# Shorter decay scans, 112-row loads, and eight small steps moved from VectorE to ScalarE and TensorE in a three-layer kernel

## The chip, the cores and the metric

The kernel runs on one core of a Trainium2 chip. Its time is the device time of one execution in microseconds; a run gives several, and the median is quoted. One execution was also recorded by the hardware profiler. The engines are TensorE (PE in the rows; PEld is its weight loading), VectorE (DVE), ScalarE (ACT), GpSimd (POOL) and SyncE (SP); each works through its own queue in order and waits for others by semaphores. SyncE and GpSimd issue the transfers here.

## The reference

```
for t in range(S):                     # layer 1: B=4, H=8, S=768, D=48
    state = alpha[t] * state + outer(k[t], v[t])
    y[t]  = q[t] @ state
x     = y, heads side by side          # [4, 768, 384]
theta = x @ w_theta                    # layer 2
u     = x + w_tok_r @ (x * cos(theta)) + w_tok_i @ (x * sin(theta))
x     = u + relu(u @ w_ch)
h     = relu(x @ w_in)                 # layer 3: 1024 columns
g, v  = h[:, :512], h[:, 512:]
v_s   = w_spatial @ normalise(v) + b_spatial
out   = (g * v_s) @ w_out
```

## The kernel before

The sequence is cut into units of 128 positions, six for each of four batches, so 24 units; a unit holds two chunks of 64 positions, and four pairs of heads lie side by side in the partitions (2 x 48 of 112 rows). For each unit, layer 1 is done in chunk form. `load_al` and `load_qk` bring the decays and q, k; `load_v` brings v. `att_scan` (L357 to L361) makes running products of the decays with two scans, one backwards into `rt` and one forwards in place, each over the 8 x 67 = 536 columns of a line in which a fixed column separates the groups; a reciprocal between them sets the forward scan's starting values. `att_qk` multiplies q and k by these products. TensorE then makes the products inside a chunk (`att_a`, tiles `psa`), which VectorE masks into `ax` and `am` (`att_mask`); `ax` is moved to the other half of the partitions by two transfers into `ay`. `att_k` and `att_kt` turn k, `att_u` makes each chunk's addition to the state, `att_y` the output. The state goes through VectorE chunk by chunk: `att_s` (L434) scales it by the chunk's decay (`ss` <- `tmp`), `att_t` (L447) adds the new part (`tmp` <- `psu`, `ss`). From unit 6 on `att_y` of a unit and `att_u` of the next are one joined TensorE step (`psuy`).

Layer 2 follows unit by unit. `tr_p` turns the output, `th_p` makes theta in turns (`th`, a PSUM tile). `th_k` (L541, ScalarE) adds a magic number that rounds to whole turns (`kk`), `th_r` (L551, VectorE) takes them off (`r`), and `th_a` and `th_s` (ScalarE) make the absolute value, sine and cosine (`z`). `z_m` multiplies them by x; for unit 0 it writes `zs` itself (L572), and that unit's accumulation uses unsplit f32 operands (`wf`). `tokmix` (L610) adds a unit's part to the five accumulators `acc0` to `acc4` of its batch; `acc1` is shared by two pieces and is set to zero first (`acc_zero`, L619). When a batch is complete, `ch_p` and its neighbours do the channel product. Layer 3 comes after unit 23.

Large operands are split into a high and a low part in a 32-bit matmul format. The weights come as 64-bit numbers in pieces (`raw`, two buffers, issued by GpSimd at first), and each piece passes ScalarE (`top`, writes `zeros`), VectorE (`join`, writes `wf`, L248), ScalarE (`high`, L259) and VectorE (`low`, L267). A new piece is loaded when a `raw` buffer has been joined.

All steps of all three layers stand in one hand-set sequence: `ORDER` is a table of step numbers, and each engine's queue is that sequence cut down to its own steps. The code also holds switches that were empty before: `THP` is a set of units for which `th_n`, `th_m` and the negated identity replace `th_r`.

## Time and profile before

| | us |
|---|---|
| median of 3 runs | 585.23 |
| lowest, highest | 584.65, 585.68 |
| profiled execution, its own time | 585.29 |
| its span in the trace | 583.5 |
| TensorE busy | 561.5 (96%) |
| VectorE busy | 440.3 (75%) |
| ScalarE busy | 252.5 (43%) |

The time of an execution is a little longer than the span of its instructions. Busy time of an engine is the time in which at least one of its instructions is recorded as running; matmuls are pipelined, so their records overlap and a busy TensorE may still be waiting a little inside. A share over the whole span mixes the three layers, so the stretches matter more than the total. The granted TensorE clock was 1.00, 2.4 GHz, in the whole span.

### The profile page before, as it was taken

The page shows a single profiled execution, that of the slowest core. Times are in us where ns is not written, and L with a number is a line of the kernel's source. Part 1 is how long each engine was busy: PE and PEld are TensorE (multiplying, and loading weights), DVE is VectorE, ACT ScalarE, POOL GpSimd, SP SyncE. Part 2 cuts the span into 40 slices and gives each one's busy share as a digit, 9 for nine tenths or more (in the row PEclk, how much of TensorE's full clock was granted, in tenths as well). Part 3 has the DMA queues.
Part 4 walks back from the last instruction along what each step waited for, and adds up shares of the span by engine and source line. Part 5 has one row for each costly group of instructions (what it writes and reads, how often), then busy time and mean ns, then how long its engine had stood idle before and what let it go on. Part 6 is the DMA issues. An engine that isn't in the chain of part 4 may idle for free.

```text
span 583.5 us, 13445 instructions
## 1 busy us (share of the span) xinstructions
PE 561.5 (96%) x5737; PEld 510.4 (87%) x5737; DVE 440.3 (75%) x769; ACT 252.5 (43%) x474; POOL 25.1 (4%) x45
## 2 busy tenths in 40 slices
PE   1799999999999999999999999999999999999997
PEld 1666878888988889988989899999999899989997
DVE  6999999988788876878756887776665775767470
ACT  2476755435335433334554443534323441343232
POOL 1101100000000000000000100000000100011000
PEclk9999999999999999999999999999999999999999
DMA  8878756363253324333344525001002010211002
GB/s 287 295 240 278 245 184 215 112 198 126 86 169 110 104 88 128 122 104 97 95 139 168 180 89 183 1 0 62 20 2 95 29 41 0 82 42 40 1 1 81
DMA packets 28220, 66.23 MB, mean 114 GB/s; under 512 B 3073, under 2 KB 14337, under 8 KB 27905
## 3 DMA queue, kind: packets, MB, share of 16 engines
q1 hardware_dynamic: 25984, 53.51, 27.7%
q0 software_dynamic: 2176, 11.86, 5.9%
q8 instruction: 45, 0.74, 0.5%
q14 instruction: 15, 0.11, 0.1%
HBM read 52.78 MB, written 9.44 MB: 107 GB/s over the span
## 4 chain that ended last, share of the span: by engine, by line
PE 79%; DVE 10%; DMA 4%; ACT 2%; issue 2%; POOL 1%; DVEq 0%; SPq 0%; POOLq 0%; ACTq 0%
PE acc L610 22%; PE acc L929 11%; PE pu L861 8%; PE psc L652 7%; PE po L987 7%; PE psv L788 6%; PE sp L900 4%; PE th L534 3%; PE psuy L466 3%; DMA raw<-in_w 3%; PE th L537 2%; PE psa L383 2%; PE psuy L424 2%; PE psk L407 1%; DVE wf L248 1%
## 5 line engine op out<-in xcount | busy, mean ns | idle before, releaser
L610 PE MATMUL acc<-w,zs 128*128 128x256 f32 (+1 forms) x828 | 165.2, 344 | 0.0
L610 PEld LDWEIGHTS acc<-w,zs 128*128 128x128 f32 x828 | 128.0, 188 | 15.4
L788 PE MATMUL psv<-w,xs 128*128 128x512 f32 x216 | 53.7, 395 | 0.0
L987 PE MATMUL po<-w,gs 128*128 128x384 f32 x288 | 52.8, 338 | 0.3 <-ACT v L799 0.3
L861 PE MATMUL pu<-xs,w 128*128 128x384 f32 x288 | 53.0, 336 | 0.0
L987 PEld LDWEIGHTS po<-w,gs 128*128 128x128 f32 x288 | 50.7, 188 | 1.6 <-ACT v L799 0.7
L861 PEld LDWEIGHTS pu<-xs,w 128*128 128x128 f32 x288 | 50.3, 188 | 0.7 <-ACT o L997 0.2
L788 PEld LDWEIGHTS psv<-w,xs 128*128 128x128 f32 x216 | 40.0, 187 | 8.2 <-ACT v L799 0.2
L652 PE MATMUL psc<-us,wch 128*128 128x384 f32 (+1 forms) x243 | 41.2, 320 | 0.0
L652 PEld LDWEIGHTS psc<-us,wch 128*128 128x128 f32 x243 | 37.8, 189 | 0.8
L541 ACT ACTIVATE kk<-th,magic 128x384 f32<-128x384 f32 x24 | 13.9, 578 | 53.3 <-PE th L537 53.3
L973 ACT CAST gs<-t 128x384 fp32r<-128x384 f32 x32 | 15.8, 513 | 48.3 <-DVE t L966 48.3
L811 POOL TENSOR_TENSOR rs<-rs,mhalf 128x1 f32<-128x1 f32 x24 | 15.6, 652 | 441.7 <-DVE rs L808 441.7
L357 DVE TENSOR_TENSOR_SCAN al<-al,heads 112x536 f32<-112x536 f32 x24 | 30.5, 1270 | 3.3 <-DMA al<-in_al 3.3
L534 PE MATMUL th<-wth,xh 128*128 128x384 f32 x144 | 31.1, 352 | 0.9 <-ACT xh L501 0.5
L361 DVE TENSOR_TENSOR_SCAN al<-al,heads 112x536 f32<-112x536 f32 x24 | 30.6, 1275 | 0.8
L369 DVE TENSOR_TENSOR qk<-qk,al 112x1024 f32<-112x1024 f32 x24 | 29.3, 1220 | 2.1 <-DMA qk<-in_qk 2.1
L929 PE MATMUL acc<-w,mx 128*128 128x384 f32 x162 | 30.7, 338 | 0.0
L929 PE MATMUL acc<-wt,vns 128*128 128x384 f32 x162 | 30.7, 338 | 0.0
L929 PEld LDWEIGHTS acc<-wt,vns 128*128 128x128 f32 x162 | 28.6, 188 | 0.1
L929 PEld LDWEIGHTS acc<-w,mx 128*128 128x128 f32 x162 | 28.6, 188 | 0.0
L534 PEld LDWEIGHTS th<-wth,xh 128*128 128x128 f32 x144 | 25.4, 194 | 2.6 <-ACT xh L501 2.0
(122 smaller groups left out, 977.5 us busy)
## 6 DMA issues: line engine op xcount, KB each, us to landing
qk<-in_qk SPq DMA_DIRECT2D x24, 512.0 KB, 4.7
raw<-in_w POOLq DMA_DIRECT2D x14, 772.0 KB, 6.4
...
raw<-in_w SPq DMA_DIRECT2D x6, 772.0 KB, 5.5
...
```

The source lines that it names most:

```text
L357: nc.vector.tensor_tensor_scan(out=back[:, ::-1], data0=line[:, ::-1], data1=one[:, ::-1], initial=1.0, op0=ALU.mult, op1=ALU.add)
L361: nc.vector.tensor_tensor_scan(out=line, data0=line, data1=one, initial=0.0, op0=ALU.mult, op1=ALU.add)
L369: nc.vector.tensor_tensor(out=x, in0=x, in1=st[u]["ar"], op=ALU.mult)
L466: nc.tensor.matmul(psy[par][64 * c:64 * c + 64, a, :], w, v, start=part == 0 or first, stop=part == 1,)
L534: nc.tensor.matmul(th, xh[:, 0, k], wth[:, pr, k], start=(k == 0 and pr == 0), stop=False)
L610: nc.tensor.matmul(acc[b, n][:, c0:c1], zs[:, pl, ri, m * 128:(m + 1) * 128], w[:, pr, t0:t1], start=first and n != 1, stop=last, skip_gro ...
L652: nc.tensor.matmul(ps, wch[:, pl, k, m * 128:(m + 1) * 128], us[:, pr, k], start=(n == 0), stop=(n == 3 * KD - 1),)
L788: nc.tensor.matmul(ps, xs2[:, pl, k, o:o + 128], win[pr, "v"][:, k], start=(n == 0), stop=(n == 3 * KD - 1),)
L861: nc.tensor.matmul(pu, win[f // 2][:, pl, k * 256 + f % 2 * 128:k * 256 + f % 2 * 128 + 128], xq[b, h][:, pr, k], start=(n == 0), stop=(n ...
L900: nc.tensor.matmul(sp[:, :TH], vns[b, s][:, pl, f * 128:(f + 1) * 128], wsp[s][:, pr, t], start=(n == 0), stop=(n == 3 * NS - 1),)
L929: nc.tensor.matmul(g, left(b, n, j, pl, c), right(n, j, pr), start=(n in (1, 5, 6) and i == 0), stop=(i == 3 * NJ - 1), skip_group_check=n ...
L987: nc.tensor.matmul(po, gs[b][:, pl, f, s * 128:(s + 1) * 128], wo[f // 2][:, pr, f % 2 * DM:(f % 2 + 1) * DM], start=(n == 0), stop=(n == ...
```

## The change

- A line of decays has 66 columns a group instead of 67, with the separating column at the end of one group and the start of the next. The scans leave out one column at the edge and run over 8 x 66 - 1 = 527 columns.
- `load_al` and `load_qk` bring 112 rows instead of 128; the rest of the tile was never read.
- `SA`: the four state scalings of units 1 and 2 are made by ScalarE, each as four instructions of 112x48 with the decay as scale, instead of one VectorE instruction of 112x192.
- `ZA`: `acc1` is set to zero by ScalarE (scale 0.0 on the identity matrix) instead of by VectorE, for all four batches.
- `THP = (0, 1)`: for units 0 and 1 ScalarE takes the magic number off `kk` (`th_n`), and TensorE adds the negated identity times `kk` to `th` in PSUM (`th_m`, one f32 matmul of 384 columns), from which ScalarE then reads. VectorE's `th_r` is gone for them. ScalarE makes the negated identity once (`negate`).
- `ORDER` is another sequence throughout.

```diff
@@ -33,7 +33,7 @@
 NS = S // 128
 NP = H // 2
 NU = B * NS
-SEG = 67
+SEG = 66
 QOFF, KOFF, AOFF = 0, 512, 1024
 ALINE = 544
 KD = DM // 128
@@ -60,11 +60,13 @@
 EARLY = {'a': 3, 'u': 3, 'y': 0, 'k': 3, 't': 0, 'h': 0}
 BANKS = {'a': [0, 2], 'u': [3, 4], 'k': [3]}
 UY = tuple(range(6,23))
-THP = ()
+THP = (0,1)
 STP = ()
 STILL = ()
 WT = 0
 WM = 1
+ZA = 1
+SA = ((1, 0), (1, 1), (2, 0), (2, 1))
 NQ = 16
 QKB = 3
 ALB = 2
@@ -76,56 +78,56 @@
 
 
 ORDER = [int(n) for n in """
-129 0 163 130 164 66 131 6 165 132 133 67 138 68 134 139 167 166 11 69 140 7 141 70 202 135 8 137 168 1 9 203 136 12 142 169 10 176 173 13 170 16 174
...
+130 131 67 0 7 166 132 167 206 133 168 134 68 139 69 135 169 12 70 140 165 141 8 136 71 138 142 137 9 205 170 10 2 13 11 171 143 178 175 172 14 174
...
 """.split()]
 
 
@@ -189,7 +191,7 @@
     NB = 2
     heads = pa.tile([112, 8, SEG], F32, name="heads")
     nc.vector.memset(heads, 0.0)
-    nc.vector.memset(heads[:, :, 0:1], 1.0)
+    nc.vector.memset(heads[:, :, SEG - 1:SEG], 1.0)
 
     steps = {}
     runs = {}
@@ -336,15 +338,15 @@
     def load_al(u):
         t = pa.tile([128, 2 * 8 * SEG + 4], F32, tag="al", name="al", bufs=ALB)
         st[u]["al"], st[u]["rt"] = (t[:112, n:n + 8 * SEG].rearrange("p (g j) -> p g j", g=8) for n in (0, 8 * SEG))
-        st[u]["ar"] = t[:112, 2:2 * 8 * SEG + 4].rearrange("p (c x) -> p c x", c=2)[:, :, :8 * SEG].rearrange(
+        st[u]["ar"] = t[:112, 1:2 * 8 * SEG + 3].rearrange("p (c x) -> p c x", c=2)[:, :, :8 * SEG].rearrange(
             "p c (g j) -> p c g j", g=8
         )[:, :, :, :64]
-        nc.sync.dma_start(t[:, :8 * SEG], al_in[u, :, :8 * SEG])
+        nc.sync.dma_start(t[:112, :8 * SEG], al_in[u, :, :8 * SEG])
 
     def load_qk(u):
         t = pa.tile([128, AOFF], F32, tag="qk", name="qk", bufs=QKB)
         st[u]["qk"] = t[:112]
-        nc.sync.dma_start(t, qk_in[u])
+        nc.sync.dma_start(t[:112], qk_in[u])
 
     def load_v(u):
         v = pa.tile([128, 3, NP, D], F32, tag="vd", name="vd", bufs=NB)
@@ -355,14 +357,15 @@
         al, rt = st[u]["al"], st[u]["rt"]
         line, back, one = (x.rearrange("p g j -> p (g j)") for x in (al, rt, heads))
         nc.vector.tensor_tensor_scan(
-            out=back[:, ::-1], data0=line[:, ::-1], data1=one[:, ::-1], initial=1.0, op0=ALU.mult, op1=ALU.add
+            out=back[:, :0:-1], data0=line[:, :0:-1], data1=one[:, :0:-1], initial=1.0, op0=ALU.mult, op1=ALU.add
         )
-        nc.vector.reciprocal(out=al[:, :, 1:2], in_=rt[:, :, 2:3])
-        nc.vector.tensor_tensor_scan(out=line, data0=line, data1=one, initial=0.0, op0=ALU.mult, op1=ALU.add)
+        nc.vector.reciprocal(out=al[:, :, 0:1], in_=rt[:, :, 1:2])
+        n = 8 * SEG - 1
+        nc.vector.tensor_tensor_scan(out=line[:, :n], data0=line[:, :n], data1=one[:, :n], initial=1.0, op0=ALU.mult, op1=ALU.add)
 
     def decay(u, c):
         rt = st[u]["rt"].rearrange("p (a c) j -> p a c j", c=2)
-        return rt[:, :, c, 2:3].to_broadcast([112, NP, D])
+        return rt[:, :, c, 1:2].to_broadcast([112, NP, D])
 
     def att_qk(u):
         x = st[u]["qk"].rearrange("p (c g j) -> p c g j", c=2, g=8)
@@ -431,6 +434,11 @@
     def att_s(u, c):
         ss = st[u]["ss", c] = pa.tile([112, NP, D], F32, tag="ss", name="ss", bufs=SSB)
         tmp = st[u]["psu", 0][:112] if c and summed(u) else tmps.pop(0)
+        if (u, c) in SA:
+            rt = st[u]["rt"].rearrange("p (a c) j -> p a c j", c=2)
+            for a in range(NP):
+                nc.scalar.activation(ss[:, a], tmp[:, a], AF.Identity, scale=rt[:, a, c, 1:2])
+            return
         nc.vector.tensor_tensor(out=ss, in0=tmp, in1=decay(u, c), op=ALU.mult)
 
     def summed(u):
@@ -616,7 +624,11 @@
 
     def acc_zero(b):
         acc[b, 1] = accp.tile([128, 512], F32, tag="acc1", name="acc1")
-        nc.vector.memset(acc[b, 1], 0.0)
+        if ZA:
+            out = acc[b, 1].rearrange("p (a c) -> p a c", a=4)
+            nc.scalar.activation(out, ident[:, None, :].to_broadcast([128, 4, 128]), AF.Identity, scale=0.0)
+        else:
+            nc.vector.memset(acc[b, 1], 0.0)
 
     def evac(b, m):
         x = xT[b]
@@ -1077,7 +1089,7 @@
             ss = [("ss", SSB, (u, c))] if i or c else []
             k = None
             if ss:
-                k = at(f"s{c}", "dve" if c and mine else "dve*", 0.27, att_s, c, after=[ksc, ktx, kfirst if c and mine else None], tiles=[al, *ss, *tmps_in])
+                k = at(f"s{c}", *(("act", 0.6) if (u, c) in SA else ("dve" if c and mine else "dve*", 0.27)), att_s, c, after=[ksc, ktx, kfirst if c and mine else None], tiles=[al, *ss, *tmps_in])
                 kss.append(k)
             if c == 0 and mine:
                 ktx = at("t0", "pe", 0.33, att_i, after=[k, ku, ("load_cst",)], tiles=[ps("u", 0), *ss]) if i else ku
@@ -1129,7 +1141,7 @@
                 )
         if i:
             continue
-        step(0.0, "dve", 0.41, acc_zero, b, tiles=[ta[1]])
+        step(0.0, *(("act", 0.5) if ZA else ("dve", 0.41)), acc_zero, b, after=[("load_cst",)], tiles=[ta[1]])
 
     for b in range(B):
         u = b * NS + NS - 1
@@ -1374,9 +1386,10 @@
     qk[:, :, :, :D, KOFF:] = k.reshape(B, NS, 2, D, 512)
     e = np.ones((B, NS, 2, 64, NP, 2, SEG), q.dtype)
     e[..., 0] = 0.0
-    e[:, :, :, :D, :, :, 2:66] = al
-    line = np.zeros((NU, 128, ALINE), q.dtype)
-    line[:, :, :8 * SEG] = e.reshape(NU, 128, 8 * SEG)
+    e[..., SEG - 1] = 0.0
+    e[:, :, :, :D, :, :, 1:65] = al
+    line = np.zeros((NU, 112, ALINE), q.dtype)
+    line[:, :, :8 * SEG] = e.reshape(NU, 128, 8 * SEG)[:, :112]
     v = f["v"].reshape(B, NP, 2, NS, 2, 64, D).transpose(0, 3, 2, 5, 4, 1, 6)
 
     vt = v.reshape(NU, 128, DM)
@@ -1387,7 +1400,7 @@
     cst[:64, 128:] = m
     cst[64:, 128:] = m
     return {
-        "al": line, "qk": qk.reshape(NU, 128, 1024), "v": np.concatenate([vt, vn], axis=2), "cst": cst,
+        "al": line, "qk": qk.reshape(NU, 128, 1024)[:, :112], "v": np.concatenate([vt, vn], axis=2), "cst": cst,
         "w64": _pieces(f), "w_sp": f["moe2_w_spatial"].T, "b_sp": f["moe2_b_spatial"],
     }
 
```

VectorE's queue just ahead of the first product `zs` of x with sine and cosine (`SCALAR_TENSOR_TENSOR al` are the scans, `ss` the state scalings, `tmp` the state additions, `r` theta's turns). Before:

```order
L369 TENSOR_TENSOR qk<-qk,al 112x1024
L391 TENSOR_TENSOR ax<-acc_379,cst_sb 128x256
L391 TENSOR_TENSOR am<-acc_380,cst_sb 128x256
L551 SCALAR_TENSOR_TENSOR r<-kk,th 128x384
L519 TENSOR_TENSOR xh<-pst,xh 128x384
L447 TENSOR_TENSOR tmp<-acc_408,ss 112x192
L248 SCALAR_TENSOR_TENSOR wf<-raw,zeros 128x768
L434 TENSOR_TENSOR ss<-tmp,al 112x192
L572 SCALAR_TENSOR_TENSOR zs<-z,x 128x768
```

And now:

```order
L250 SCALAR_TENSOR_TENSOR wf<-raw,zeros 128x768
L455 TENSOR_TENSOR tmp<-acc_399,ss 112x192
L372 TENSOR_TENSOR qk<-qk,al 112x1024
L527 TENSOR_TENSOR xh<-pst,xh 128x384
L455 TENSOR_TENSOR tmp<-acc_400,ss 112x192
L394 TENSOR_TENSOR ax<-acc_421,cst_sb 128x256
L250 SCALAR_TENSOR_TENSOR wf<-raw,zeros 128x768
L580 SCALAR_TENSOR_TENSOR zs<-z,x 128x768
```

The turns `r`, a mask and the two scalings of unit 2 are gone from ahead of `zs`, and both additions of unit 2 stand there.

ScalarE's queue over the same place, from the second unit's `x` (`zeros` is a weight's first step, `kk` the magic step and the unmagic step, `xT` and `xh` the turned output). Before:

```order
L411 COPY kt<-acc_354 128x448
L482 COPY x<-psy 128x4x48 x2
L239 ACTIVATE zeros<-raw 128x768
L541 ACTIVATE kk<-th,magic 128x384
L501 CAST xh<-pst 128x384
L506 COPY xT<-pst 128x3x128
L556 ACTIVATE kk<-r 128x384
L566 ACTIVATE z<-r 128x384
L563 ACTIVATE z<-kk,halfpi 128x384
```

And now:

```order
L1021 ACTIVATE negative<-cst_sb 128x128
L440 ACTIVATE ss<-tmp,al 112x48 x4
L414 COPY kt<-acc_357 128x448
L241 ACTIVATE zeros<-raw 128x768
L549 ACTIVATE kk<-th,magic 128x384
L509 CAST xh<-pst 128x384
L552 ACTIVATE kk<-kk,unmagic 128x384
L514 COPY xT<-pst 128x3x128
L440 ACTIVATE ss<-tmp,al 112x48 x4
L241 ACTIVATE zeros<-raw 128x768
L564 ACTIVATE kk<-th 128x384
L574 ACTIVATE z<-th 128x384
```

Unit 2's scalings stand on both sides of unit 0's theta; the second comes behind one weight's `zeros`, `kk`, the unmagic step and `xT`.

TensorE's queue from unit 3's turned k and the second theta up to the output of unit 2. Before:

```order
L407 MATMUL psk<-cst_sb,qk 128x112 x4
L534 MATMUL th<-wth,xh 128x384 x6
L537 MATMUL th<-wth,xh 128x384 x3
L383 MATMUL psa<-qk 64x64 x16
L610 MATMUL acc_497<-wf,zs 128x512
L610 MATMUL acc_104<-wf,zs 128x256
L610 MATMUL acc_507<-wf,zs 128x512
L610 MATMUL acc_508<-wf,zs 128x256
L466 MATMUL psy<-ss,qk 64x48 x4
```

And now:

```order
L555 MATMUL th<-kk,negative 128x384
L542 MATMUL th<-wth,xh 128x384 x6
L410 MATMUL psk<-cst_sb,qk 128x112 x4
L545 MATMUL th<-wth,xh 128x384 x3
L386 MATMUL psa<-qk 64x64 x16
L618 MATMUL acc_512<-wf,zs 128x512
L618 MATMUL acc_160<-wf,zs 128x256
L555 MATMUL th<-kk,negative 128x384
L474 MATMUL psy<-ss,qk 64x48 x4
```

The two products with `negative` stand ahead of the second theta and behind the first accumulation, and the second accumulation has moved behind unit 2's output.

SyncE's queue starts with the decays, the first `qk` and the constants, where it was decays, constants and `qk`, and the third `qk` stands right behind the second; before, the decays of unit 2 and the first transfers of `ax` stood between them.

## Rows read from the trace of the kernel before

**Rows 1.** Page parts 1 and 2: busy us, share, count; busy tenths in 40 slices.

```profile
PE 561.5 (96%) x5737; PEld 510.4 (87%) x5737; DVE 440.3 (75%) x769; ACT 252.5 (43%) x474; POOL 25.1 (4%) x45
...
DVE  6999999988788876878756887776665775767470
```

**Rows 2.** Windows table: stretch and length, busy us of each engine (count), clock, DMA.

```profile
9.70:37.00 27.30, 20.52 (x377) 17.23 (x377) 25.61 (x41) 14.24 (x26) 3.16 (x6) 1.00 0.81 272
37.00:88.70 51.70, 50.23 (x698) 39.37 (x698) 50.32 (x78) 35.86 (x64) 4.24 (x8) 1.00 0.70 238
88.70:312.70 224.00, 223.99 (x3193) 200.03 (x3193) 179.35 (x286) 98.72 (x193) 0.00 (x0) 1.00 0.40 127
312.70:580.00 267.30, 266.55 (x1473) 253.76 (x1472) 179.82 (x355) 100.62 (x189) 15.56 (x24) 1.00 0.16 57
```

**Rows 3.** TensorE's waits up to 90: us, times, longest us.

```profile
PE acc L407 <- DVE qk L369: 9.7, 1, 9.7
...
PE th L534 <- DVE r L551: 0.3, 1, 0.3
```

**Rows 4.** Chain of waits up to 100: start us, us, what.

```profile
13.67 0.86 DVE w L267
...
32.91 0.42 ACT kk L541
...
36.10 5.33 DMA al<-in_al
...
46.26 0.27 DVE ss L434
...
80.99 0.46 DVE r L551
...
87.72 1.06 PE acc L610 x6
```

**Rows 5.** Timeline of VectorE up to 48: start us, us, instruction, idle before.

```profile
1.62 0.48 DVE L619 MEMSET acc<- 128x512 f32 x1
...
3.53 1.27 DVE L357 TENSOR_TENSOR_SCAN al<-al,heads 112x536 f32<-112x536 f32 x1 [1.17 <-DMA al<-in_al]
...
8.43 1.23 DVE L369 TENSOR_TENSOR qk<-qk,al 112x1024 f32<-112x1024 f32 x1 [2.08 <-DMA qk<-in_qk]
...
33.37 0.56 DVE L551 SCALAR_TENSOR_TENSOR r<-kk,th 128x384 f32<-128x384 f32 x1 [0.48 <-ACT kk L541]
...
35.99 0.95 DVE L572 SCALAR_TENSOR_TENSOR zs<-z,x 128x768 f32<-128x768 f32 x1
```

**Rows 6.** Windows table for line 357 alone, up to 88.7.

```profile
0.00:88.70 88.70, 10.17 (x8) 1.00 0.74 252
```

**Rows 7.** DMA issues from 1.6 to 2.0: count, KB each, us to landing.

```profile
qk<-in_qk SPq DMA_DIRECT2D x1, 512.0 KB, 6.7
```

**Rows 8.** Timeline of ScalarE up to 42.

```profile
2.04 0.20 ACT L177 ACTIVATE mhalf<-halfpi 128x1 f32<-128x1 f32 x1
8.62 1.07 ACT L239 ACTIVATE zeros<-raw 128x768 f16<-128x768 bf16 x1 [6.38 <-DMA raw<-in_w]
...
21.84 0.54 ACT L482 COPY x<-psy 128x192 f32<-128x192 f32 x2 [2.27 <-PE psy L466]
...
31.83 1.08 ACT L239 ACTIVATE zeros<-raw 128x768 f16<-128x768 bf16 x1 [2.38 <-DMA raw<-in_w]
...
33.96 0.55 ACT L556 ACTIVATE kk<-r 128x384 f32<-128x384 f32 x1
...
35.31 0.54 ACT L411 COPY kt<-psk 128x448 f32<-128x448 f32 x1
```

**Rows 9.** DMA issues from 18.5 to 19.3.

```profile
raw<-in_w POOLq DMA_DIRECT2D x1, 772.0 KB, 6.6
```

**Rows 10.** Timeline of TensorE from 36.5.

```profile
36.99 2.85 PE L610 MATMUL acc<-wf,zs 128*128 128x512 f32 x8 [0.42 <-DVE zs L572]
39.77 0.43 PE L466 MATMUL psy<-ss,qk 48*64 48x48 f32 x5
```

2 lines of the change are left out of this document (1 added, 1 removed), and 98 rows, old and new, of the table ORDER.

## The prediction

> **What bounds the kernel now.** I read the busy shares and the forty slices first: TensorE is busy 96% of the span, so a saving on VectorE (75%) can count only where TensorE waits for it [rows 1]. The table of stretches says where that is. From 88.7 to 580 TensorE is idle for 0.76 us out of 491.3; VectorE has a fifth of that time free or more. Up to 88.7 it is the other way round: VectorE is busy 50.32 of 51.70 us between 37.0 and 88.7, and TensorE idles for 6.8 us between 9.7 and 37.0 [rows 2], after 9.7 us at first, which the list of its waits puts on the first decayed `qk` [rows 3]. The chain of waits runs through VectorE's steps and decay loads and has TensorE's accumulations from 87.72 on [rows 4]. So the kernel is a head of 88.7 us paced by VectorE and a rest in which TensorE works without a break. What the change is worth is how much earlier the head ends, plus or minus TensorE work added or pushed into the rest. The mark that I use is the joined step of unit 6 at 88.70.
>
> **VectorE's part of the sum.** Before that mark the change takes from VectorE four state scalings, at 0.27 us in the chain (0.35 each alone, but neighbours overlap) [rows 4]: 1.08 us. It takes two turns (`r` of units 0 and 1), 0.46 us each in the chain [rows 4]: 0.92. Each scan loses 9 of 536 columns; at 1271 ns for 536 (10.17 us for eight) that is 21 ns, and 16 scans stand before the mark, two for each of eight units: 0.34 [rows 6]. The zeroing of `acc1` for batch 0 saves nothing: it ran at 1.62, while VectorE waited for the first decay load until 3.53 [rows 5]; the other three lie in TensorE's stretch. Sum: 2.34. The order also pushes one weight's low part past the mark (0.86 in the chain, `w` at 13.67 [rows 4]), to where VectorE has slack. VectorE could reach the mark 3.2 us sooner.
>
> **The start.** The first `qk` now goes out second instead of third and has 112 rows; it was 6.7 us on its way, and VectorE waited 2.08 us for it [rows 5, 7]. Gained there: between 0 and those 2.08, and I expect about 0.7 (0.45 from the place in the queue, the rest from bytes). But the next VectorE step needs `zeros` from ScalarE, which began at 8.62 when its weights landed and took 1.07 [rows 8], so VectorE starts that join near 9.7 as before. TensorE's first matmuls come sooner, VectorE's stream does not: 0 to 0.4, taken as 0. Smaller decay and qk loads save some 100 KB a unit next to 772 KB for a weight piece [rows 9]; I count nothing for it.
>
> **ScalarE's part.** It gets four scalings of four instructions (112x48), the removal of the magic number twice, one negation and the zeroing. For a 48-column scaling the nearest rows are 203 ns for one column and 0.54 us for a pair of 192 columns [rows 8]: between 0.2 and 0.27 each, so 0.8 to 1.1 per scaling; I take 0.8. That is 3.2 us plus two of about 0.45 and some 0.7 for negation and zeroing: 4.8 us more on an engine that was busy 50.1 of 79 us between 9.7 and 88.7 [rows 2]. It has room; the question is the wait. Unit 2's scalings stand between two additions on VectorE. Between those additions the new order leaves VectorE a `qk` (1.2, as the one at 8.43) and an `xh` of the size of a turn (0.46), 1.6 us of cover against 0.8 plus a hop of 0.04 (the first `kk` ends at 33.33, `r` starts at 33.37 [rows 4, 5]). Unit 1 has more cover. Against that, the second scaling stands in ScalarE's queue behind `kk`, `xh`, the unmagic step and `xT`, and unit 2's first addition waits for TensorE, which has to be earlier too. New waits on VectorE: between 0 and 2.6 (four times 0.9 less 0.27, with no cover at all); I take 0.7, because the cover is there in the written order but the queue ahead is longer than it was.
>
> The Trainium skill ("ScalarE: Activation LUTs", What ACT_TABLE_LOAD costs) prices an ACTIVATE at 186 ns plus 0.833 ns a column, 93 ns more for each pointer operand, with 93 ns of overlap back to back. By that, as an estimate, a scaling would be about 0.9 us instead of 0.8, and the four 0.4 us more on ScalarE in all. No row here has a 48-column scaling with a pointer, so that figure is open; the sum above would stay as it is as long as the cover holds.
>
> **TensorE's part.** Two matmuls of 384 f32 columns are added. The eight f32 records at 36.99 cover 1536 columns in 2.78 us, since the next step starts at 39.77 [rows 10]: 1.81 ns a column, 0.70 us each, 1.39 for both. The first falls before the second theta, where TensorE waited anyway [rows 3]; the second comes after the first accumulation. In exchange one accumulation step (1.06 [rows 4]) that stood before the mark now stands behind it. Up to the mark TensorE has 0.33 us more to do and had 17.9 us of idle time [rows 2, 3]; I let it follow VectorE. In the rest it has the same steps as before plus that accumulation: 1.06 us lost again.
>
> **Sum.** The mark comes 3.2 - 0.7 = 2.5 us sooner, the rest takes 1.06 longer: 1.44 us less. Against the profiled execution's own 585.29 (span 583.5 and 1.8 around it) this is 583.8. The median of the three runs is 585.23, 0.06 away, so the number stands for it too. About 0.2%, 1.2 us, is what a measurement of this kernel can tell from no change. The order of the rest has been rewritten as well, with the same steps; idle time like the 0.76 us there [rows 2] can come or go: 0.5 either way.
>
> **Rivals.** First, **TensorE takes it back**. Between 37.0 and 88.7 TensorE idles only 1.5 us by the records [rows 2]. If the rest of its time there is work that does not shrink, only what VectorE gains up to the first `zs` counts. That is 1.08 for the scalings and 0.46 for one `r`; a mask that moves behind `zs` and an addition that moves ahead of it, both of about a scaling's size, cancel. 1.5, less the 0.7 of waits, is 0.8. The second theta matmul, 0.70, then eats it: 585.2, between 584.6 and 585.7. For it speaks that TensorE is recorded as busy 97% there; against it that the chain goes through VectorE still at 80.99 and reaches TensorE's accumulations at 87.72 alone [rows 4].
>
> Second, slower: **ScalarE's queue becomes the chain**. In the new order the magic step, the unmagic step and the last scaling of unit 2 all stand behind one weight's `zeros` activation. Before, such an activation waited 2.38 us for its weights and began at 31.83 [rows 8]. If it is as late now, it ends at 32.9; `kk`, `xh`, the unmagic step and `xT` at 0.42 each (as `kk` in the chain) and the scaling 0.8 follow: 35.4. Another `zeros` (1.08), the absolute value, sine and cosine (1.35 together, from 33.96 to 35.31) bring `zs` to 37.8 instead of 35.99 [rows 4, 5, 8]; with the second added matmul the head ends 1.8 + 0.7 later, and the decay load of unit 4, which started at 36.10 after the last scaling of unit 2 and took until 41.43 [rows 4], is no earlier either. VectorE's remaining relief, `r` of unit 1 (0.46), is all that is set against it: 587.3. It decides from where that weight lands after about 30 (35.99 less the 4.9 from that `zeros` to `zs` and its own 1.08). In the new order it is the piece ahead of that one, which was issued near 19 and 6.6 on its way [rows 9], so it landed near 25.6; that speaks against it.
>
> Third, **the loads do not get lighter**: 112 rows could be spread over fewer transfer engines than 128 were. Were it half as many, the packets of a load would take twice as long; the decay load of 5.33 us would hold its scan by as much again [rows 4]: 585.3 + 5.3, 590.6, from that load alone. All loads of this trace have 128 or 64 rows, so no row excludes it. By the Trainium skill ("DMA: Bandwidth & Descriptors", Why a DMA increments its semaphore by 16 and not by 1) a load takes the largest number of engines up to 16 that divides its rows, which for 112 is still 16; that speaks against this rival.
>
> **Chances.** Forecast (582.4 to 584.0): 0.60. TensorE takes it back: 0.22. ScalarE's queue: 0.15. Loads: 0.03. The range: its low end is the forecast without new waits (3.2 + 0.4 - 1.06 = 2.54 less, 582.75) and 0.3 for the rewritten rest, 582.4. Its high end takes in the whole first rival and the near part of the second, up to 586.2; about 0.07 are left below and 0.12 above. Faster by over 0.2% (under 584.0): 0.60. Within 0.2%: 0.22. Slower: 0.18, the second and third rival.
>
> **What would show it.** In the profile of the changed kernel the joined step of unit 6 should begin near 86.2, the first `zs` near 35.1, and VectorE should not wait over 1 us in all at unit 1's and 2's additions. A scaling should take 0.8 to 1.1 from its first start to its last end. The two added matmuls should span 0.6 to 0.75 each. TensorE's steps after the mark should take as long as before plus 1.06. It is wrong if the first `zs` starts after 36, if VectorE waits for ScalarE at `tmp`, if a weight's `zeros` is late again in ScalarE's queue ahead of `kk`, or if the mark is earlier and the end is not.

## The result, and the profile after

The changed kernel took 590.08 us, the median of four runs (587.73 to 591.91), beside 585.45 of the kernel before in the same session: a ratio of 1.0078, with an interval of 1.0051 to 1.0106. It is slower by 0.8%. The profiled execution is the shortest of the four, 587.73, with a span of 586.0 against 583.5; so 2.5 us of span have to be found in its trace. The other executions lost more, and no trace shows where.

The page of the changed kernel: busy us of each engine (as [rows 1]), and the granted TensorE clock in 40 slices, in tenths:

```profile
PE 563.0 (96%) x5741; PEld 512.2 (87%) x5741; DVE 436.2 (74%) x759; ACT 260.4 (44%) x497; POOL 25.5 (4%) x45
...
PEclk9979999999999999999999999999999999999999
```

VectorE has 4.1 us less to do than before over the whole span; that went as meant. The stretches, cut at the joined step of unit 6, which begins at 89.53 now and began at 88.70 before, first of the kernel before, then of the changed one (stretch and length; busy us and count of TensorE, its weight loads, VectorE, ScalarE, GpSimd; clock; DMA share; GB/s):

```profile
0.00:88.70 88.70, 70.74 (x1074) 56.60 (x1074) 81.14 (x129) 52.65 (x92) 9.52 (x21) 1.00 0.74 252
88.70:583.50 494.80, 490.72 (x4664) 453.79 (x4663) 359.17 (x641) 199.82 (x383) 15.56 (x24) 1.00 0.27 89
```

```profile
0.00:89.53 89.53, 70.88 (x1072) 57.00 (x1073) 76.53 (x119) 57.27 (x111) 9.51 (x21) 0.96 0.79 241
89.53:586.00 496.47, 492.08 (x4670) 455.17 (x4669) 359.64 (x641) 203.11 (x387) 16.01 (x24) 1.00 0.28 85
34.80:41.60 6.80, 6.63 (x45) 4.29 (x45) 5.58 (x11) 4.07 (x7) 0.53 (x1) 0.50 0.78 260
```

Read VectorE's busy time (third) against the length of the first stretch: 81.14 of 88.70 before, 76.53 of 89.53 after. **VectorE does 4.61 us less work up to the mark and idles 5.44 us more, 13.00 instead of 7.56**; the mark is 0.83 later. The rest, to the end of the span, is 1.67 us longer (496.47 against 494.80). The third row of the changed kernel is a stretch in which TensorE was granted 0.50 of its clock, 1.2 GHz (the `7` in the slices). The kernel before shows no such stretch; that its clock was 1.00 in the whole span, as the section on the profile before has it, does not hold, and the section on the clock below says why.

VectorE's waits between 3 and 92, before and after (what waits, for whom; us in all, times, longest):

```profile
DVE qk L369 <- DMA qk<-in_qk: 2.1, 1, 2.1
DVE al L357 <- DMA al<-in_al: 1.4, 2, 1.2
DVE wf L248 <- ACT zeros L239: 0.9, 1, 0.9
DVE tmp L447 <- PE acc L424: 0.7, 1, 0.7
DVE r L551 <- ACT kk L541: 0.5, 1, 0.5
DVE xh L519 <- ACT xT L506: 0.2, 1, 0.2
```

```profile
DVE wf L250 <- ACT zeros L241: 4.5, 3, 1.9
DVE al L359 <- DMA al<-in_al: 3.6, 3, 1.4
DVE qk L372 <- DMA qk<-in_qk: 1.0, 1, 1.0
DVE am L394 <- PE psa L386: 0.9, 1, 0.9
DVE ax L394 <- PE acc L386: 0.5, 1, 0.5
```

The list grew from 5.8 to 10.5 us. The waits for the first `qk`, for `kk` (theta's turns) and at the state additions (`tmp`) are gone or smaller, as the change meant them to be. In their place stand waits for a weight piece's words (`zeros`, 3.6 us more), for decay loads (2.2 more), for a later `qk` load and for TensorE. Where they are, in VectorE's timeline of the changed kernel (start, length, instruction, idle before it; [rows 5] of before):

```profile
6.55 1.22 DVE L372 TENSOR_TENSOR qk<-qk,al 112x1024 f32<-112x1024 f32 x1
9.66 0.96 DVE L250 SCALAR_TENSOR_TENSOR wf<-raw,zeros 128x768 uint32<-128x768 uint32 x1 [1.89 <-ACT zeros L241]
...
19.39 0.96 DVE L250 SCALAR_TENSOR_TENSOR wf<-raw,zeros 128x768 uint32<-128x768 uint32 x1 [1.02 <-ACT zeros L241]
...
28.24 1.25 DVE L359 TENSOR_TENSOR_SCAN al<-al,heads 112x527 f32<-112x527 f32 x1 [1.01 <-DMA al<-in_al]
...
33.17 1.23 DVE L372 TENSOR_TENSOR qk<-qk,al 112x1024 f32<-112x1024 f32 x1 [1.03 <-DMA qk<-in_qk]
...
36.25 0.95 DVE L580 SCALAR_TENSOR_TENSOR zs<-z,x 128x768 f32<-128x768 f32 x1
38.07 0.42 DVE L394 TENSOR_TENSOR am<-psa,cst_sb 128x256 f32<-128x256 f32 x1 [0.87 <-PE psa L386]
...
42.59 1.26 DVE L359 TENSOR_TENSOR_SCAN al<-al,heads 112x527 f32<-112x527 f32 x1 [1.25 <-DMA al<-in_al]
...
81.81 0.96 DVE L250 SCALAR_TENSOR_TENSOR wf<-raw,zeros 128x768 uint32<-128x768 uint32 x1 [1.64 <-ACT zeros L241]
```

The first `zs` begins at 36.25, against 35.99. Three of these waits can be followed in the chain of waits (as [rows 4]):

```profile
23.33 1.02 ACT ss L440 x4
24.74 8.34 DMA qk<-in_qk
...
34.32 0.56 DVE xh L527
34.97 0.98 PE psk L410 x4
...
36.69 5.88 DMA al<-in_al
...
72.50 8.12 DMA raw<-in_w
```

ScalarE scales unit 1's second state from 23.33 to 24.35 (four instructions, `x4`). Right behind its end SyncE issues the decay load of unit 3, at 24.37, and behind that `qk` of unit 3, at 24.74; this holds VectorE and then, through `xh` and the keys of unit 3 (`psk`), TensorE. The loads issued between 24 and 25.5 (count, KB, us to landing):

```profile
raw<-in_w POOLq DMA_DIRECT2D x1, 772.0 KB, 8.5
qk<-in_qk SPq DMA_DIRECT2D x1, 448.0 KB, 8.3
al<-in_al SPq DMA_DIRECT2D x1, 231.0 KB, 3.9
```

The same `qk` load, issued at 23.90 in the kernel before, landed in 3.8 us. The next row of the chain is the decay load of unit 4, issued at 36.69 (36.10 before, [rows 4]). The last is a weight piece; ScalarE empties its words from 80.69 on, and VectorE's join at 81.81 has waited 1.64 for them. It is the last long wait ahead of the mark.

ScalarE's timeline has the scalings, and the emptying of a weight piece's words (`zeros`) that VectorE waits for (compare [rows 8]):

```profile
8.55 1.07 ACT L241 ACTIVATE zeros<-raw 128x768 f16<-128x768 bf16 x1 [6.32 <-DMA raw<-in_w]
...
23.33 1.01 ACT L440 ACTIVATE ss<-tmp,al 112x48 f32<-112x48 f32 x4
...
28.13 1.09 ACT L241 ACTIVATE zeros<-raw 128x768 f16<-128x768 bf16 x1
```

TensorE's timeline has the two added matmuls with the negated identity (L555; each is recorded as two, `x2`), the second in the stretch of half the clock:

```profile
30.57 0.91 PE L555 MATMUL th<-kk,negative 128*128 128x384 f32 x2 [0.21 <-ACT kk L552]
...
40.65 1.30 PE L555 MATMUL th<-kk,negative 128*128 128x384 f32 x2
```

### The profile page after: what moved, and what is told of

The parts are those of the page before. It is cut to its first block, busy times and chain, and to the rows that moved or that the text cites. A ratio compares the mean times of both kernels' runs of the same rounds, so it can differ in the third digit from the quotient of the medians.

```text
span 586.0 us, 13497 instructions
## 1 busy us (share of the span) xinstructions
PE 563.0 (96%) x5741; PEld 512.2 (87%) x5741; DVE 436.2 (74%) x759; ACT 260.4 (44%) x497; POOL 25.5 (4%) x45
## 4 chain that ended last, share of the span: by engine, by line
PE 85%; DVE 5%; DMA 5%; issue 1%; ACT 1%; SPq 0%; DVEq 0%; ACTq 0%; POOLq 0%
PE acc L618 23%; PE acc L941 11%; PE po L999 9%; PE psv L800 9%; PE pu L873 9%; PE psc L664 7%; PE sp L912 4%; PE th L542 3%; PE psuy L474 3%; DMA raw<-in_w 2%; PE th L545 2%; PE psa L386 2%; PE psuy L427 2%; DMA qk<-in_qk 1%; PE psk L410 1%
## 5 line engine op out<-in xcount | busy, mean ns | idle before, releaser
L664 PEld LDWEIGHTS psc<-us,wch 128*128 128x128 f32 x243 | 37.8, 189 | 0.6
L359 DVE TENSOR_TENSOR_SCAN al<-al,heads 112x527 f32<-112x527 f32 x24 | 30.0, 1249 | 5.8 <-DMA al<-in_al 5.8
L941 PE MATMUL acc<-w,mx 128*128 128x384 f32 x162 | 31.2, 338 | 0.0
L364 DVE TENSOR_TENSOR_SCAN al<-al,heads 112x527 f32<-112x527 f32 x24 | 30.1, 1256 | 0.8
L241 ACT ACTIVATE zeros<-raw 128x768 f16<-128x768 bf16 (+1 forms) x22 | 22.9, 1040 | 11.5 <-DMA raw<-in_w 11.4
```

The lines of the kernel that those rows point to most:

```text
L241: nc.scalar.activation(out, c["top"].rearrange("p (c k) -> p c k", k=4)[:, :, 0], AF.Identity, scale=0.5)
L359: nc.vector.tensor_tensor_scan(out=back[:, :0:-1], data0=line[:, :0:-1], data1=one[:, :0:-1], initial=1.0, op0=ALU.mult, op1=ALU.add)
L364: nc.vector.tensor_tensor_scan(out=line[:, :n], data0=line[:, :n], data1=one[:, :n], initial=1.0, op0=ALU.mult, op1=ALU.add)
L664: nc.tensor.matmul(ps, wch[:, pl, k, m * 128:(m + 1) * 128], us[:, pr, k], start=(n == 0), stop=(n == 3 * KD - 1),)
L941: nc.tensor.matmul(g, left(b, n, j, pl, c), right(n, j, pr), start=(n in (1, 5, 6) and i == 0), stop=(i == 3 * NJ - 1), skip_group_check=n ...
```

## The experiments

All ratios are to the kernel before in the same session. "Mark" is the begin of the joined step of unit 6 in the profiled execution, "waits" the sum of VectorE's waits between 3 and 92 there (before: 88.70 and 5.8); two profiled executions of one kernel (the 527-column runs) had marks 0.5 apart. "Clock" is the mean granted clock over all executions (before: 0.998). The mark and the waits are those of one execution each, and the ratios do not follow them: 87.61 and 91.22 go with 1.0032 and 1.0031.

| kernel | ratio | interval | mark | waits | clock |
|---|---|---|---|---|---|
| changed kernel | 1.0078 | 1.0051–1.0106 | 89.53 | 10.5 | 0.995 |
| changed, 128-row loads | 1.0031 | 1.0001–1.0061 | 91.22 | 11.5 | 0.996 |
| changed, early loads put back, 128 rows | 1.0077 | 1.0059–1.0095 | 90.05 | 11.1 | 0.993 |
| changed, with filler matmuls | 1.0074 | 1.0044–1.0105 | 91.68 | 12.5 | 0.998 |
| new order, 527 columns, nothing else | 1.0032 | 1.0011–1.0054 | 87.61 | 6.0 | 0.993 |
| changed, steps of the head mended | 1.0066 | 1.0049–1.0083 | 95.66 | 14.9 | 0.995 |
| the same with 128 rows | 1.0059 | 1.0045–1.0073 | 90.83 | 11.5 | 0.993 |
| all parts, new order up to the mark | 1.0054 | 1.0037–1.0071 | 90.19 | 10.2 | 0.997 |
| all parts, new order behind the mark | 1.0057 | 1.0035–1.0078 | 90.26 | 9.4 | 0.998 |
| all parts, old order | 1.0032 | 1.0017–1.0046 | 91.38 | 10.3 | 0.999 |
| all parts but the rows, old order | 1.0012 | 0.9999–1.0025 | 89.53 | 8.4 | 0.999 |
| before, 112-row loads | 1.0014 | 1.0003–1.0025 | 90.03 | 7.1 | 0.999 |
| before, 112 rows as 64 + 48 | 1.0108 | 1.0088–1.0129 | 93.76 | 11.2 | 0.999 |
| before, 527 columns | 0.9985, 0.9997 | 0.9968–1.0002, 0.9981–1.0014 | 87.71, 87.19 | 5.3, 4.6 | 0.999, 0.997 |
| before, scalings on ScalarE | 0.9998 | 0.9986–1.0010 | 89.41 | 6.8 | 0.999 |
| the same, decays copied out | 0.9987 | 0.9974–1.0001 | 89.13 | 7.0 | 1.000 |
| before, turns by TensorE | 1.0001 | 0.9986–1.0017 | 89.49 | 7.4 | 0.998 |
| before, scalings and turns left out | 0.9959 | 0.9945–0.9972 | 88.04 | 6.9 | 0.999 |

### The 112-row loads

The changed kernel with 128 rows, and the kernel before with 112:

```diff
-        nc.sync.dma_start(t[:112, :8 * SEG], al_in[u, :, :8 * SEG])
+        nc.sync.dma_start(t[:, :8 * SEG], al_in[u, :, :8 * SEG])
...
-        nc.sync.dma_start(t[:112], qk_in[u])
+        nc.sync.dma_start(t, qk_in[u])
```

> The changed kernel with its two loads back at 128 rows. Theory R (the 112-row loads are slower: packets of the changed kernel's trace took 226 ns for 4096 bytes against 179 before, and its loads held VectorE for 1.0, 1.0 and 1.25 us): this comes back to about 585 to 586, mean packet near 180 ns. Theory O (the new order places loads and weights so that they collide, and the rows do not matter): 588 to 591, packets as slow as in the changed kernel.

> The kernel before with 112-row loads alone; scans, order and engines as before. Theory R: slower than before by 2 to 5 us, 587 to 590, with 4096-byte packets over 210 ns in the head. Theory O: same as before or up to 0.5 us faster, 584.9 to 585.4.

Undoing the rows in the changed kernel gives back 0.47 points of the 0.78; adding them to the kernel before costs 0.14, with an interval above 1 (1.0003 to 1.0025). All parts in the old order gave 1.0032 with 112 rows and 1.0012 with 128, the mended order 1.0066 and 1.0059 (both below). The four pairs go the same way, by 0.07 to 0.47 points, though within three of them the intervals overlap. So 112 rows cost, and the gain in bytes is none. The transfers up to 88.7, before and with 112 rows alone (packets, MB, share of 16 engines, of all that SyncE issued; then issues, KB each, median us to landing):

```profile
q1 hardware_dynamic: 4887, 10.34, 34.6%
...
qk<-in_qk SPq DMA_DIRECT2D x9, 512.0 KB, 5.4
```

```profile
q1 hardware_dynamic: 4589, 9.42, 38.0%
...
qk<-in_qk SPq DMA_DIRECT2D x9, 448.0 KB, 6.9
```

0.92 MB fewer take 38.0% of the engines' time instead of 34.6%: 4.03% a megabyte instead of 3.35, a fifth more. That holds in all four pairs: 3.95 to 4.08 with 112 rows, 3.31 to 3.36 with 128. The packets of 4096 bytes, which are the rows of `qk`, took 226 to 236 ns in the mean in every kernel that loads 112 rows at once, and 168 to 183 in every kernel that loads 128. The time to landing does not show it so plainly: 6.9 against 5.4 us here, but 6.6 against 6.9 in the changed order, 6.2 against 6.8 with all parts in the old order and 8.1 against 6.8 in the mended one. The records don't tell which of the 16 engines carried a packet, so why the packets are slower stays open. One idea was that 112 rows are dealt out unevenly and that loads of 64 and 48 rows would not be:

```diff
-        nc.sync.dma_start(t, qk_in[u])
+        for a, b in ((0, 64), (64, 112)):
+            nc.sync.dma_start(t[a:b], qk_in[u, a:b])
```

> The kernel before with 112-row loads, each issued as two transfers of 64 and 48 rows; so the same bytes as with one 112-row transfer, and twice the issues on SyncE. Theory M (it is the shape of 112 rows in one transfer that makes its packets slow, 236 ns for 4096 bytes against 179): packets near 180 ns and 585.2 to 585.9. Theory B (any load that leaves out the last 16 rows is slow): packets over 210 ns and 586.3 to 587.5.

They are worse still, 1.0108; VectorE's waits are 11.2 us instead of 7.1 with one load of 112 rows, the packets of `qk` 265 ns. Splitting also doubles the number of issues on SyncE's queue, so this run shows only that splitting is no cure.

### All parts in the old order, and the new order without the parts

The sequence of the kernel before, with the new steps at their places (in names of steps, for unit 0; unit 1 likewise; the second of the two runs has loads of 128 rows):

```diff
 tr_h.0
+negate
...
 th_k.0
+th_n.0
...
-th_r.0
+th_m.0
```

> All parts of the change (527-column scans, 112 rows, scalings and zeroing on ScalarE, two theta turns by TensorE) in the order of before; the added steps stand where the step they replace stood. Theory O (order at fault): 583.5 to 585. Theory R (rows at fault): 588 to 591. Theory S (the scalings on ScalarE hold the decay buffer and so the loads, whatever the order): 586.5 to 589 and VectorE waits for decay loads of units 3 and 4.

> All parts of the change but the 112-row loads, in the order of before (scalings and zeroing on ScalarE, two turns by TensorE, 527-column scans). The same with 112 rows took 587.9, and the scalings alone and the turns alone changed nothing. If the rows carry that loss: 585.4 to 586.2. If the scalings and the turns get in each other's way on ScalarE: 586.8 to 587.8, with VectorE's wait for xT near 2.9 us again.

And the changed kernel's sequence with 527 columns and 128 rows, in which VectorE keeps the scalings, the turns and the zeroing:

```diff
-THP = (0,1)
+THP = ()
...
-ZA = 1
-SA = ((1, 0), (1, 1), (2, 0), (2, 1))
+ZA = 0
+SA = ()
```

> The new order and the 527-column scans, with 128-row loads, scalings, zeroing and turns on VectorE as before; the steps stand where their replacements stood. Theory O: 587 to 591, with the gap of TensorE before the second theta that the changed kernel has. Theory R: 585 to 586. Theory S: 585 to 586, without the waits for the decay loads of units 3 and 4.

The changed kernel loses 0.78 points, its parts in the old order 0.32, those without the rows 0.12: so parts and order both cost. The new order without the moved steps loses 0.32 although its profiled execution has an early mark, 87.61; its times spread from 584.94 to 590.67. With the moved steps and the same 128 rows it is 1.0031: in the new order, too, what the moved steps give or take can't be told from nothing.

This run also tells which waits belong to the order. In it VectorE does the scalings itself and the decay load of unit 3 goes out at 22.73, earlier than in the changed kernel (24.37) and in the kernel before (23.47). The scans of units 3 and 4 wait for their loads all the same:

```profile
27.34 1.26 DVE L359 TENSOR_TENSOR_SCAN al<-al,heads 112x527 f32<-112x527 f32 x1 [1.02 <-DMA al<-in_al]
...
41.18 1.26 DVE L359 TENSOR_TENSOR_SCAN al<-al,heads 112x527 f32<-112x527 f32 x1 [1.41 <-DMA al<-in_al]
```

The changed kernel has 1.01 and 1.25 there. So these waits come with the new sequence and not with the scalings on ScalarE. The waits for a piece's words do not: they are 1.3 us in all here, against 4.5 in the changed kernel and 6.2 in the same with 128 rows.

### Why the moved steps gain nothing

Each hand-over alone in the old order, first the scalings, then the turns; and the same steps left out altogether (the states of units 1 and 2 are not decayed; the sines and cosines of units 0 and 1 are of numbers near zero; four additions write into the buffers of `ss` instead of the single `tmp`):

```diff
+        if (u, c) in SA:
+            for a in range(NP):
+                nc.scalar.activation(ss[:, a], tmp[:, a], AF.Identity, scale=rt[:, a, c, 2:3])
+            return
```

> The kernel before with the four scalings on ScalarE alone; the order, loads and scans as before. Theory S (the scalings on ScalarE cost): a scaling takes about 1.0 us there, stands behind other work and holds the decay buffer, so the time rises by 0.8 to 1.5 us to about 587. Theory T (VectorE's relief counts): falls by 0.5 to 1.0 us, 585.0 to 585.5. Theory D (transfers set the head): within 0.5 us of before, since VectorE waits for transfers in the place of the scalings.

```diff
-THP = ()
+THP = (0, 1)
```

> The kernel before with theta's turns of units 0 and 1 by TensorE alone. Theory S2 (the turn through ScalarE's unmagic step and TensorE is a longer chain than VectorE's one instruction): slower by 0.5 to 1.5 us, since ScalarE and TensorE each stand once more in the way of the first sine. Theory T: 0.3 to 0.9 faster. Theory D: within 0.5.

```diff
+        if u in (1, 2):
+            st[u]["ss", c] = tmps.pop(0)
+            return
...
+        if u < 2:
+            st[u]["r"] = st[u]["kk"]
+            return
```

> The kernel before with the four scalings of units 1 and 2 and the two turns of units 0 and 1 left out and nothing in their place (so unit 1's and 2's state is not decayed and two units' sines and cosines are of small numbers): 2.0 us less on VectorE in the head, nothing more on another engine, loads and order as before. The forecast's step (VectorE's relief counts in full): 2.0 us faster, 583.5 to 584.3. Theory D (VectorE then waits for transfers): 0 to 0.8 us faster, and VectorE's waits for decays and weights up to 88 grow by over 1 us.

Left out, the steps are worth 0.41 points, 2.4 us (1.6 to 3.2), against 2.0 in the sum (four scalings 1.08, two turns 0.92). Handed over, the four scalings give 0.02 points and the turns -0.01. For the turns VectorE's timeline of that run shows where the relief went:

```profile
35.45 0.56 DVE L519 TENSOR_TENSOR xh<-pst,xh 128x384 fp32r<-128x384 f32 x1 [2.29 <-ACT xT L506]
...
37.33 0.95 DVE L572 SCALAR_TENSOR_TENSOR zs<-z,x 128x768 f32<-128x768 f32 x1
```

VectorE no longer waits for `kk`, but 2.29 us for the turned input of unit 1, which ScalarE copies (`xT`) behind `kk` and the unmagic step; before, the same wait was 0.20. The first `zs` is 1.34 later than before (35.99, [rows 5]).

For the scalings, look at when the decay load of unit 3 goes out (start and length on SyncE's queue), in the kernel before, with scalings on ScalarE, and with them left out:

```profile
23.47 0.33 SPq L342 DMA_DIRECT2D al<-in_al  x1
```

```profile
25.15 0.33 SPq L343 DMA_DIRECT2D al<-in_al  x1
```

```profile
20.90 0.58 SPq L342 DMA_DIRECT2D al<-in_al  x1
```

The decay tile has two buffers. Its last reader is the scaling of the unit two back, and when that moves to ScalarE the load goes out 1.68 us later, and the `qk` load behind it in SyncE's queue with it. Left out, it goes out 2.57 us earlier. So the run without the steps has more than one relief at once, VectorE's and that of the buffers. One more run frees the decay buffer and keeps the scalings on ScalarE:

```diff
+        if (u, 0) in SA:
+            st[u]["dec"] = pa.tile([112, 8, 1], F32, tag="dec", name="dec", bufs=2)
+            nc.vector.tensor_copy(out=st[u]["dec"], in_=rt[:, :, 2:3])
...
-            rt = st[u]["rt"].rearrange("p (a c) j -> p a c j", c=2)
+            rt = st[u]["dec"].rearrange("p (a c) j -> p a c j", c=2)
```

> The kernel before with the four scalings on ScalarE and nothing else, but the eight decays that they read of units 1 and 2 are first copied by VectorE into a tile of their own (two copies of 112x8, about 0.2 us each as the reciprocals of that size), so that the decay buffer is free as soon as VectorE has used it. Theory F (the scalings on ScalarE gain nothing because they hold the decay buffer, and with it the fourth decay load and the query load behind it): that load goes out at 19 to 22 us instead of 25.2 in the run with the scalings on ScalarE and 23.5 in the kernel before; VectorE has 1.08 - 0.42 = 0.66 us less to do and waits no more than before; 0.996 to 0.999 of the kernel before. Rival S (the way through ScalarE itself is what gives the time back: unit 2's additions and the turn behind ScalarE's longer queue): the load goes out earlier all the same, the time is 0.9995 to 1.0015, as without the copies (0.9998, 0.9986 to 1.001).

```profile
19.97 0.58 SPq L343 DMA_DIRECT2D al<-in_al  x1
```

The load goes out at 19.97, and the time is 0.9987 with an upper end at 1.0001: in theory F's span, and told neither from no change nor from the 0.9998 of the run without the copies. That the moved scalings hold the load back is shown; that this costs time is not.

### The clock, and the early loads

In the changed kernel TensorE was granted half its clock for 6.8 us from 34.80 on, after it had waited 2.4 us ahead of `psk`; the second matmul with the identity takes 1.30 us there and the first, at full clock, 0.91. A filler keeps TensorE busy ahead of that place:

```diff
+        if u == 3:
+            for _ in range(4):
+                nc.tensor.matmul(acc[0, 1][:, :384], nil, wth[:, 0, 0].bitcast(F32), start=False, stop=True, skip_group_check=True)
```

> The changed kernel with four f32 matmuls of zeros (0.64 us each, 2.6 in all, added to an accumulator that holds zeros) ahead of unit 3's turned k, where TensorE paused from about 32.1 to 35.0 in the changed kernel's trace and its granted clock fell to 0.50 from 34.80 for 6.83 us. Theory C (the pause lets the clock fall, and the matmuls after it at the lower clock cost 2 to 3 us): the clock stays at 1.00 in that stretch, the first accumulation takes 1.4 instead of 2.72 us, and the time falls by 1 to 2.5 us against the changed kernel's 590.1. Theory D (transfers alone set the head; what TensorE does there is hidden): no change, or up to 0.5 slower.

There the second matmul now takes 0.81, and a stretch at 0.50 came later, from 47.2 on for 3.4 us. The ratio stayed, 1.0074. The three executions with a granted clock of 1.000 took 587.3, 588.7 and 589.7, so the loss is there without a low clock. The clock may have some weight all the same: over 123 executions of the kernel before the time rises with the missing clock (correlation 0.57), and within all kernels together by 0.25 us for each 0.001 of mean clock. That is a correlation: a stall may cause both the low clock and the time.

The mean clock also leaves something out. The trace's records of the clock begin at 31.63 in the kernel before and at 27.98 in the changed one, and the views count a time without a record as 1.00. The same 32 matmuls of one unit, before, on either side of 31.63:

```profile
30.32 1.13 PE L383 MATMUL acc<-qk 48*64 48x64 f32 x32
...
35.82 0.76 PE L383 MATMUL psa<-qk 48*64 48x64 f32 x32
```

In the changed kernel they take 1.14 us at 16.79 and again 1.14 at 36.87, in the stretch granted 0.50. So TensorE ran at the pace of the half clock up to the first record in both kernels. Counted so, half-clock time ahead of the mark is 31.6 us before, 34.8 (27.98 and 6.83) in the changed kernel, and 31.2 (20.91 and 10.24) in the new order with 527 columns alone, whose mean clock of 0.993 looks like a loss. These are single executions, but they forbid pricing the loss by the mean clock.

The new order also issues `qk` of unit 2 and `v` of units 2 and 3 earlier. Put back, with 128 rows:

```diff
 load_qk.1
-load_qk.2
...
 load_al.2
+load_qk.2
...
-load_v.2
...
 load_qk.3
-load_v.3
+load_v.2
...
 move_a.2
+load_v.3
```

> The changed kernel with 128-row loads and with three early loads put back where the order of before has them (the third qk behind the first transfers of ax, v of units 2 and 3 behind the loads they had overtaken). Theory L (the new order's loss is its early loads, which collide with weight pieces): 585 to 586.5, less spread than the 585 to 592 of the same kernel without this edit, and VectorE waits for weights' first steps under 3 us instead of 6.2. Theory Q (it is the new order on VectorE and ScalarE, which puts steps that need a load or a weight ahead of work that could cover them): 587.5 to 589 with the same waits.

1.0077, against 1.0031 with the early loads and the same 128 rows: early loads in the way of others are not the reason.

### Which half of the order, and can it be mended

All parts, the changed kernel's sequence up to the joined step of unit 6 and the old one behind it, and the mirror of that; here the seam of the first, against the changed kernel:

```diff
 load_al.8
+low.2
+load_qk.9
+tokmix.4.2.0
+att_t.6.1
+high.11
+z_m.5
 att_uy.6
```

> All the parts of the changed kernel, with 112-row loads; up to the joined step of unit 6 in the changed kernel's order, from there on in the order of the kernel before. Theory H (the first 90 us of the new order cost the time): as the changed kernel, 1.006 to 1.009 of the kernel before. Rival R (the rest of the new order costs it): as the parts in the old order, 1.002 to 1.004. The mark of unit 6 stands near 89.5 by either, since the steps ahead of it are those of the changed kernel; what tells them apart is the time from there to the end, 496.5 us in the changed kernel's trace.

> The mirror of the run before: the old order up to the joined step of unit 6, then the changed kernel's order, all parts with 112-row loads. Theory H: 1.002 to 1.004 of the kernel before. Rival R: 1.006 to 1.009. If both hybrids lose as much as the changed kernel, neither half of the order carries the loss alone.

1.0054 and 1.0057, midway between the parts in the old order (1.0032) and the changed kernel (1.0078): **by the middle values neither theory holds alone, and each half of the new order costs about 0.2 points**. The four intervals overlap, so this is the likeliest reading and not a shown one. In the profiled executions the stretch behind the mark takes 495.81 and 495.74 us, against 495.11 with all parts in the old order. Then the changed kernel with a few steps moved, with 112 and with 128 rows; the first of the moves:

```diff
 att_k.0
-join.13
 att_a.0
 att_scan.1
+att_kt.0
+acc_zero.0
+att_u.0
+join.13
+att_s.0.1
+load_al.2
 raw_f64.2
 high.13
-att_kt.0
-acc_zero.0
-att_u.0
```

> The changed kernel with a few steps of its first 45 us in another place: the scan of unit 1 ahead of the first joining, the first keys and the first state ahead of the first high part on ScalarE, the scaling of unit 0 right after the first joining and the load of unit 2's decay behind it; the joining of the third piece behind the scan of unit 2; the emptying of the fourth piece's words ahead of unit 2's scaling on ScalarE; the low part of unit 1's turned input ahead of unit 3's query step; the load of unit 4's decay ahead of the mask loads. Theory Q (VectorE's steps stand ahead of what they wait for, and that is where the relief went): VectorE's waits in the first 90 us fall from 10.5 us to 5 to 8, the mark of unit 6 goes from 89.5 to 86.5 to 88.5, and the time to 0.999 to 1.005 of the kernel before. Rival: the waits only move on, since what they wait for (loads and ScalarE) is what sets the head; waits stay at 9 to 11 us, the mark near 89.5, the time at 1.006 to 1.009.

> The same mended order with loads of 128 rows. Theory Q: 0.994 to 1.001 of the kernel before, the one that may beat it; rival: as the changed kernel with 128 rows, 1.000 to 1.006.

Theory Q falls: 1.0066 and 1.0059. Waits rose to 14.9 us and the mark went to 95.66 in an execution of 593.14, the longest of its six; with 128 rows they are 11.5 and 90.83. What the steps put ahead now wait for, in VectorE's timeline of the mended kernel:

```profile
11.07 1.25 DVE L359 TENSOR_TENSOR_SCAN al<-al,heads 112x527 f32<-112x527 f32 x1 [3.50 <-DMA al<-in_al]
...
32.49 1.25 DVE L359 TENSOR_TENSOR_SCAN al<-al,heads 112x527 f32<-112x527 f32 x1 [3.93 <-DMA al<-in_al]
```

The scan of unit 1 takes the place of the joining that waited for `zeros`, and waits 3.50 us for its own load. In the changed kernel that load, issued at 2.13, is this long on its way:

```profile
al<-in_al SPq DMA_DIRECT2D x1, 231.0 KB, 8.1
```

It lands near 10.2, just after the words of the first piece (8.55 and 1.07). So up to about 10 us VectorE waits for a load in either order.

### The shorter products

```diff
-SEG = 67
+SEG = 66
...
+        n = 8 * SEG - 1
+        nc.vector.tensor_tensor_scan(out=line[:, :n], data0=line[:, :n], data1=one[:, :n], initial=1.0, op0=ALU.mult, op1=ALU.add)
```

> The kernel before with the 527-column scans alone (66 columns a group), all else as before. 16 scans in the head lose 21 ns each, so VectorE has 0.34 us less. Theory T (VectorE's relief counts where nothing is handed over): 0.2 to 0.4 us faster. Otherwise no change. It is below what the runs can tell surely, so the trace's mark at unit 6 counts as well.

> The kernel before with running products of 527 columns alone, timed a second time: it is the only part so far whose middle value lies below the kernel before (0.9985, 0.9968 to 1.0002), and the only candidate for a version faster than both. If the shorter products count in full (0.34 us ahead of the mark, VectorE pacing), 0.9994 of the kernel before; if the lower middle value is noise, 1.000; if the first run's value holds, 0.9985.

0.9985 and 0.9997: both below 1, neither told from no change, and 0.9994 (the 0.34 us of the sum) lies in both intervals. No version that does all of the work beats the kernel before by more than can be measured; this one and the copied decays come nearest.

## Why the prediction was wrong

It said 583.8 us, 582.4 to 586.2, with 0.18 for slower; 590.08 came. Step by step:

- **VectorE's relief (3.2 us)** came as work: 4.61 us less busy time up to the mark and ten instructions fewer (129 to 119): the eight that the sum names, the zeroing (0.48) among them, and two more that now stand behind the mark, a state addition and a product of x with sine and cosine. Left out without a hand-over, the scalings and turns gave 2.4 us where the sum had 2.0, in a run that frees buffers as well.
- **The new waits on VectorE (0.7, between 0 and 2.6)** is the step that failed. VectorE idles 5.44 us more, twice the upper bound. The bound was made at one place, the additions behind ScalarE's scalings, and no wait of the changed kernel's list is there: the cover held. What it put at nothing are waits for loads. VectorE now meets more weight pieces and decay loads that have not landed: waits for words emptied from a piece grew from 0.9 to 4.5 us, those for decay loads from 1.4 to 3.6. The decay loads' part comes with the new sequence, since the run without the moved steps has it too. The words' part is over 3 us only where new sequence and moved steps are together. Which of the moved steps makes it stays open, and so does why the `qk` load of unit 3 took 8.3 us and not 3.8, since a weight piece, 112 rows and the decay load fall together there. SyncE's wait for ScalarE's scaling, with 24.37 instead of 22.73 for that decay load, is one more path that the prediction did not weigh; no run shows its price.
- **What paces the head.** "A head paced by VectorE" was read from a busy share of 50.32 of 51.70. That share told that VectorE was late, and not that loads and ScalarE would be in time for an earlier VectorE. Of the 10.5 us of waits after, 9.1 are for a load or for words emptied from one (4.4 of 5.8 before).
- **The start** was right: the first `qk` now begins at 6.55 instead of 8.43, VectorE then waits for `zeros` (1.89) and joins at 9.66, "near 9.7 as before".
- **Smaller loads counted as nothing** was wrong in sign: 0.07 to 0.47 points in the four pairs of runs. The third rival had the sign and got 0.03; its mechanism was half as many engines, with packets twice as long and 5.3 us. Measured are packets of `qk` a quarter to two fifths longer. The rule of the Trainium skill ("DMA: Bandwidth & Descriptors", Why a DMA increments its semaphore by 16 and not by 1), by which 112 rows still use 16 engines, was taken to speak against the rival. The records don't show the engines, so they neither bear the rule out nor speak against it; equal engines do not mean equal speed, and the measured time a megabyte decides.
- **The price of a scaling (0.8, 0.8 to 1.1)** is 0.99 to 1.01: inside the bounds. By the figures of the Trainium skill ("ScalarE: Activation LUTs", What ACT_TABLE_LOAD costs) an instruction of 48 columns with one pointer takes 319 ns and the next can start after 226, as an estimate. The trace agrees, with 0.32 us each and starts 0.23 apart. From the first start to the last end that makes 1.0 us; the prediction's 0.9 left out the end of the last. The added matmuls, forecast at 0.70 and to span 0.6 to 0.75, span 0.91 at full clock and 1.30 mostly at half. With the six theta matmuls behind it the first takes 1.97, where six alone took 1.29 before (at 34.07): 0.68 more, by that difference, so the price was right and the sign to look for was not.
- **The rest behind the mark (+1.06)** was 1.67. TensorE's busy time there grew by 1.36 us with six matmuls more, the accumulation pushed behind the mark, which the sum has at 1.06; its idle time grew by 0.31. The remaining 0.61 is a little over the 0.5 that the prediction allowed either way.
- **ScalarE's queue becomes the chain (587.3)** is nearest in time, by another way: the weight piece that it feared late was in time (`zeros` at 28.13 without a wait), and `zs` began at 36.25 instead of its 37.8 (after 36, which the prediction named as a sign of being wrong). But its side remark, that the decay load of unit 4 is no earlier, was a place to look.

The loss of 0.78 points can be put together along two ways, and they differ. From the old order: shorter products and moved steps 0.12, the rows 0.20, the new order 0.46. From the new order: the order with the shorter products 0.32, the moved steps nothing (1.0032 without, 1.0031 with them), the rows 0.47. Both are estimates from middle values whose intervals reach 0.1 to 0.3 points to either side. Common to both is that the rows and the order cost and that the moved steps give nothing. What lengthens the executions that were not profiled, 1.6 to 4.2 us beyond the one shown, has no trace.
